# Attention and gated MLP on one core: ScalarE's work and the loads of the attention part in the order of the steps, and the chunks of last rows moved in fewer transfers

## The chip, the cores and the metric

The kernel runs on one core of one Trainium2 chip. The metric is the device time of one execution, in microseconds (us). The engines are TensorE (PE, with PEld for its weight loads), VectorE (DVE), ScalarE (ACT), GpSimd (POOL) and SyncE (SP), which here issues every DMA. Each engine works through its own list of instructions in the order in which the program was laid down for it, and waits at an instruction until what that needs is there.

## The reference

`x` is 2048 rows of 576. The reference computes

```
mod = silu(c) @ w_mod                          # six rows of 576: sa, ca, ga, sb, cb, gb
h = layernorm(x) * (1 + ca) + sa
q = h @ wq                                     # 32 heads of 128; 16 kv heads, each used by two
p = softmax(q k^T / sqrt(128)), o = p v        # k, v: the last 512 cached positions
x = x + ga * (o @ wo)
h = layernorm(x) * (1 + cb) + sb
x = x + gb * ((sigmoid(h @ w_gate) * (h @ w_up)) @ w_down)
```

All of it is float32. A product is made of split operands: each number is a rounded part (hi) and the rest (lo), and three products of parts are added.

## The kernel before, in words

The work is one long attention part and, behind it, the gated MLP. Rows stand in 4 blocks of 512, and each block in 4 tiles of 128.

**The loop of the attention part** (L708 to L724) runs over steps `n`, four for each pair of head and block, 512 steps that do scores in all. A step issues on TensorE, in this order of the code: a quarter of the q projection of a later pair (`qproj`, L337), the scores of tile n+2 (`scores`, L353), the four transposes of the probabilities of tile n (`transp`, L371), and for earlier pairs the product with `wo` (`wo_acc`, L399) and with `v` (`pv`, L384). Between them lies the chain of one tile: scores in PSUM, then DVE's row maximum (L364), ACT's exponential (L366), PE's transposes two steps on (L377), and ACT's and DVE's copies of the transposed tile as hi and lo (L380, L381). Scores and transposes share three PSUM buffers (tag `st`), so the transposes of step n+1 take the buffer that the exponential of tile n+2 has read.

**Work at given steps.** A table `at_step` gives each step further work, done ahead of the step's own (L709): loads of raw weights into four buffers (`raw`, L73); ACT's rounding of them to hi (L214 for `wq`, L239 for `wo`, L327 for `k`, L333 for `v`); POOL's lo parts (L218, L219, L243, L334) and its product of `wo` with the gate row (L433); and three times the sums for a row of `mod` (`mod_sum`, L121: ten ACT products at L126, then POOL sums). Layernorms of blocks 2 and 3 and, after the middle, of blocks 0 and 1 again also stand in this table.

**Chunks.** The MLP's weights are summed and split ahead of time in the background, in 135 chunks, one every third step: a chunk that starts at step n is loaded at n (`bg_load`), summed by POOL at n+3 (`bg_sums`), rounded by ACT at n+6 (`bg_hi`, L654), its lo part made by POOL at n+7 (`bg_lo`, L659), and stored to DRAM at n+8 (`bg_store`). There are 72 chunks "ab" of whole rows of the gate and up weights, 9 "tail" chunks with the last 32 rows of four column blocks each, and 54 "down" chunks. Their scratch lies in parts of the `x` tiles that are free at that time, three regions in turn.

**The order of the work.** A planner lays the instructions down for each engine as soon as its own model of times says that they are ready, by the order of the code where several are. `pin(i)` (L209) holds an instruction behind the one that the code issued just before it on the same engine; that one may itself be free to move. Before the change pinned are the chunks' work and the splits of `wq` and `wo`; not pinned are the loads of raw weights, the exponential, the copies at L380, L347, L394, L327 and L333, and `mod_sum`. TensorE and VectorE are not pinned in the loop in either kernel.

Of the kernel before, what the change touches and what calls it, by code (L numbers as in the profile page):

```python
# [24 lines left out]
def adaln_block_kernel(ctx: ExitStack, tc: tile.TileContext, x, k_cache, v_cache, wq, wo, w_gate, w_up, w_down,  # L25
# [54 lines left out]


# [28 lines left out]
    def mod_load(m):  # L110
        ws = []
        for j in range(2):
            w = wp.tile([P, NC, D2], F32, tag="wa", name="wm", bufs=4)
            cols = slice(m * D + j * D2, m * D + (j + 1) * D2)
            nc.sync.dma_start(w, w_mod[: NC * P, cols].rearrange("(k p) n -> p k n", p=P))
            ws.append(w)
        t = wp.tile([TAIL, D], F32, tag="h", name="wmt", bufs=4)
        nc.sync.dma_start(t, w_mod[NC * P :, m * D : (m + 1) * D])
        return ws, t

    def mod_sum(loaded):  # L121
        ws, t = loaded
        for j in range(2):
            parts = [ws[j][:, k, :] for k in range(NC)] + [t[:, j * D2 : (j + 1) * D2]]
            for k, w in enumerate(parts):
                nc.scalar.activation(w, w, AF.Copy, scale=cexp[: w.shape[0], k : k + 1])  # L126
# [16 lines left out]
    def load_x(b):  # L143
        nc.sync.dma_start(xs[b], xf[b])
# [38 lines left out]
    def ln_transpose(b, t):  # L183
# [4 lines left out]
        if b > 1:  # L188
            tc.keep_in_program_order(i)
# [6 lines left out]
        nc.scalar.activation(main[:, :NC, cols], src, AF.Copy)  # L196
        nc.vector.tensor_sub(main[:, NC:, cols], src, f32(main[:, :NC, cols]))  # L197
        nc.scalar.activation(tail[:, 0, cols], pt[:, :P], AF.Copy)
# [3 lines left out]
    def load_a(w, n0):  # L202
        raw = raw_tile([P, NC + 1, P])
        nc.sync.dma_start(raw[:, :NC, :], w[: NC * P, n0 : n0 + P].rearrange("(k p) n -> p k n", p=P))
        for s in range(2):
            nc.sync.dma_start(raw[s * TAIL : (s + 1) * TAIL, NC, :], w[NC * P :, n0 : n0 + P])
        return raw

    def pin(i):  # L209
        tc.keep_in_program_order(i)  # L210
# [21 lines left out]
    def load_b(w, n0):  # L232
        raw = raw_tile([P, D])
        nc.sync.dma_start(raw, w[n0 : n0 + P, :])
# [61 lines left out]
    NEG = {}  # L296
# [20 lines left out]
    def load_kv(cache, g):  # L317
        raw = raw_tile([P, KT, DH])
        nc.sync.dma_start(raw, cache[0, g, SK - W :, :].rearrange("(p k) d -> p k d", k=KT))
        return raw  # L320

    def prep_k(raw):
# [4 lines left out]
        nc.scalar.activation(t[:, 0, :], p, AF.Copy)  # L327
# [3 lines left out]
    def prep_v(raw):  # L331
        t = at.tile([P, 2, KT, DH], F32R, tag="vs", name="vs", bufs=2)
        nc.scalar.activation(t[:, 0], raw, AF.Copy)  # L333
# [3 lines left out]
    def qproj(b, part):  # L337
# [7 lines left out]
        if part == 3:  # L345
            t = at.tile([P, 2, BLK], F32R, tag="qt", name="qt", bufs=2)
            nc.scalar.activation(t[:, 0, :], p, AF.Copy, scale=QSCALE)  # L347
# [5 lines left out]
    def scores(n):  # L353
# [10 lines left out]
        nc.vector.tensor_reduce(NEG[b][:, i : i + 1], p, axis=AX.X, op=OP.max, negate=True)  # L364
        PP[n] = at.tile([P, W], F32, tag="pp", name="pp", bufs=2)
        nc.scalar.activation(PP[n], p, AF.Exp, bias=NEG[b][:, i : i + 1], accum_out=SUM[b][:, i : i + 1])  # L366
# [4 lines left out]
    def transp(n):  # L371
# [8 lines left out]
        nc.scalar.activation(PT[b][:, 0, :, cols], pv_, AF.Copy)  # L380
# [3 lines left out]
    def pv(b, k):  # L384
# [7 lines left out]
        if k == KT - 1:  # L392
            o = at.tile([P, 2, BLK], F32R, tag="ov", name="ov", bufs=2)
            nc.scalar.activation(o[:, 0, :], OP_[b], AF.Copy)  # L394
# [136 lines left out]
    def pair_sums(pair, t, h, ta, tb, ea, eb):  # L531
# [6 lines left out]
        for c0, src in ((0, h[0].rearrange("p (c d) -> p c d", c=2)), (2, ta), (4, h[1][:, None, hi]), (5, tb)):  # L538
            n = src.shape[1]
            nc.sync.dma_start(d[:, c0 : c0 + n, t, 0:D2], src)  # L540
            for q in range(1, 4):
                nc.sync.dma_start(d[:, c0 : c0 + n, t, 2 * P + q * TQ : 2 * P + (q + 1) * TQ], src[:, :, 2 * P :])
# [11 lines left out]
    def park_x(b):  # L554
        nc.sync.dma_start(xscr[b], xs[b])
# [12 lines left out]
    A11, A12, S1, S2, S4, S3, A22, A21 = range(8)  # L568
# [25 lines left out]
    def bg_load(k, b0):  # L594
# [16 lines left out]
        if kind == "ab":  # L611
            parts = [(slice(0, P), s * P, P, slice(f * P, (f + 1) * P))]
        else:
            parts = [(slice(q * TQ, (q + 1) * TQ), 2 * P, TQ, slice((f + q) * P, (f + q + 1) * P)) for q in range(4)]
        for rows, r0, nr, cc in parts:
            g = w_gate[:, cc].rearrange("(c r) n -> r c n", c=2)[r0 : r0 + nr]
            pin(nc.sync.dma_start(raw[rows, 0:2, :], g))
            pin(nc.sync.dma_start(raw[rows, 3, :], w_up[r0 : r0 + nr, cc]))
            pin(nc.sync.dma_start(raw[rows, 2, :], w_up[D2 + r0 : D2 + r0 + nr, cc]))
# [24 lines left out]
    def bg_pairs(k):  # L644
        r, m, hi = BG[k]
        if jobs[k][0] == "down":
            return [(0, 2, r[:, 0:2, :]), (2, 4, m[:, 0:2, :]), (4, 5, r[:, 2:3, :]), (5, 7, m[:, 2:4, :])] \
            + [(7, 8, r[:, 3:4, :])] * (jobs[k][1] == NF // 2 - 1)
        return [(0, 2, r[:, 0:2, :]), (2, 6, m), (6, 7, r[:, 2:3, :])]
# [11 lines left out]
    def bg_store(k):  # L661
        kind, f, s = jobs[k]
        hi = BG[k][2]
# [16 lines left out]
        del BG[k]  # L680
# [5 lines left out]
    for k, (n, half) in enumerate(slots):  # L686
# [4 lines left out]
        at_n(n + 8, bg_store, k)  # L691
# [16 lines left out]
    for n in range(NLO, N + 2 * TPB):  # L708
        for fn, args in at_step.pop(n, ()):  # L709
# [7 lines left out]
        if 0 <= n < N:  # L717
            transp(n)
        if ok(b - 2):
# [52 lines left out]
    for u in range(U):  # L772
        uses.append((u, 0))
        if u:
            uses.append((u - 1, 6))
        uses += [(u, a) for a in range(1, 6)]
    uses.append((U - 1, 6))
# [16 lines left out]
    WITH = {A11: 0, A12: 1, S1: 2, S2: 3, S4: 4, S3: 5, A22: 6}  # L794
# [7 lines left out]
    sd_uses = [(g, a) for g in range(GL) for a in ORDER] + [(GL, i) for i in (0, 7, 1, 4)]  # L802
# [148 lines left out]
    for u in range(U + 1):  # L951
# [23 lines left out]
        if u > 0:  # L975
# [5 lines left out]
            if g == GL:  # L981
                a, ops = (A11, ((0, A12), (7, S4))) if u % 2 else (A12, ((1, A12), (4, S4)))
# [88 lines left out]
```

## Time and profile before

| | |
|---|---|
| median of 3 runs | 3128.54 us (3126.2 to 3131.26) |
| profiled execution | 3131.72 us, span 3129.9 us, mean granted TensorE clock 0.993 |
| PE busy | 3065.7 us of the span |
| DVE, ACT, POOL busy | 2156.5, 1452.1, 1563.0 us |
| attention loop (transposes L377) | from 54.1 to 1849.4 us of the span |

The span is the time from the first to the last instruction of the profiled execution; the execution's own time is 1.8 us more. A time in the trace is counted from the span's start. A row of the timeline has start, duration, engine, line, operation, output and input; in brackets stands how long the engine sat idle before it, and what ended that. A row of waits has who waited, for whom, us in total, how often, and the longest. A row of the windows has for each engine its busy time and number of instructions in the stretch, then the granted clock of TensorE.

### The profile page before, as it was taken

The numbers are of one execution on the slowest core, as the hardware profiler recorded it, in microseconds if no ns is written. First come the engines' busy times: TensorE is split into PE (matmuls) and PEld (weight loads), VectorE is DVE, ScalarE is ACT, GpSimd is POOL, SyncE is SP. The second block draws the span as 40 slices with busy tenths as digits, with TensorE's granted clock in tenths as the row PEclk, the third lists the DMA queues.
The fourth block names the chain that finished last, engine by engine and source line by source line (L and its number), as shares of the span: only waits on it lengthen the run. The fifth ranks groups of instructions, "written<-read, shape, count | busy, mean of one in ns | idle before, by whom it ended". The sixth has DMA issues, their size and how long they took to land.

```text
span 3129.9 us, 50861 instructions
## 1 busy us (share of the span) xinstructions
PE 3065.7 (98%) x17012; PEld 2650.5 (85%) x17012; DVE 2156.5 (69%) x4202; ACT 1452.1 (46%) x3189; POOL 1563.0 (50%) x1937
## 2 busy tenths in 40 slices
PE   7999999999999999999999999999999999999998
PEld 5888888888888788888888888888888888888887
DVE  7777777777888677777777785555555665555556
ACT  4666665656555456655555543222332322322321
POOL 3666566555444336666566614554444354434444
PEclk8999999999999999999999999999999999999999
DMA  4565566555313225544444437886666776666663
GB/s 143 149 165 151 153 163 171 146 150 160 124 31 94 66 76 162 131 126 125 108 118 115 108 112 271 265 252 208 198 200 199 220 240 198 198 196 197 201 204 119
DMA packets 576740, 501.73 MB, mean 160 GB/s; under 512 B 193504, under 2 KB 456672, under 8 KB 575456
## 3 DMA queue, kind: packets, MB, share of 16 engines
q1 hardware_dynamic: 576480, 498.49, 55.3%
q8 instruction: 135, 2.21, 0.3%
q14 instruction: 125, 1.02, 0.1%
HBM read 357.83 MB, written 140.48 MB: 159 GB/s over the span
## 4 chain that ended last, share of the span: by engine, by line
PE 89%; DVE 3%; POOL 3%; DMA 2%; issue 1%; SPq 1%; ACT 1%; POOLq 0%; DVEq 0%; ACTq 0%
PE a L892 14%; PE w L251 12%; PE qp L251 12%; PE wo L251 12%; PE ot L251 10%; PE st L251 10%; PE c L892 7%; PE st L377 7%; PE b L892 4%; SPq L670 1%; DVE x L404 0%; DVE x L864 0%; DMA ts<-scr 0%; POOL hl L823 0%; PE w L762 0%
## 5 line engine op out<-in xcount | busy, mean ns | idle before, releaser
L864 DVE TENSOR_TENSOR x<-w,x 128x288 f32<-128x288 f32 x980 | 444.3, 456 | 468.3 <-PE w L251 466.4
L251 PE MATMUL wo<-wb,ov 128*128 128x288 f32 x3072 | 618.6, 309 | 4.0 <-DVE x L404 2.6
L380 ACT ACTIVATE ptt<-st 128x512 fp32r<-128x512 f32 x512 | 305.8, 597 | 616.4 <-PE st L377 616.0
L251 PEld LDWEIGHTS w<-sd,hl 128*128 128x128 f32 x3036 | 513.7, 189 | 89.4 <-POOL hl L823 4.6
L892 PE MATMUL a<-hc,sw 128*128 128x512 f32 x2016 | 583.1, 394 | 3.4 <-DVE v L1026 1.8
L251 PE MATMUL w<-sd,hl 128*128 128x288 f32 x3036 | 565.6, 296 | 3.5 <-POOL hl L823 3.1
L404 DVE SCALAR_TENSOR_TENSOR x<-wo,rs,x 128x288 f32<-128x288 f32 x1024 | 513.6, 512 | 55.8 <-PE wo L251 7.1
L364 DVE TENSOR_REDUCE neg<-st 128x1 f32<-128x512 f32 x512 | 352.7, 689 | 282.9 <-PE st L251 280.4
L251 PEld LDWEIGHTS wo<-wb,ov 128*128 128x128 f32 x3072 | 484.4, 190 | 53.8 <-DVE x L404 4.1
L251 PE MATMUL qp<-hTm,wa 128*128 128x512 f32 x1536 | 445.7, 399 | 6.6 <-DVE qt L348 4.1
L251 PE MATMUL ot<-ptt,vs 128*128 128x512 f32 x1536 | 445.0, 397 | 0.0
L251 PE MATMUL st<-kt,qt 128*128 128x512 f32 x1536 | 438.4, 393 | 2.2 <-DVE hTm L197 2.0
L892 PEld LDWEIGHTS a<-hc,sw 128*128 128x128 f32 x2016 | 355.5, 188 | 43.1 <-DVE v L1026 3.2
L381 DVE TENSOR_TENSOR ptt<-st,ptt 128x512 fp32r<-128x512 f32 x512 | 348.9, 681 | 36.2 <-ACT ptt L380 36.1
L366 ACT ACTIVATE pp<-st,neg 128x512 f32<-128x512 f32 x512 | 349.9, 683 | 37.3 <-DVE neg L364 33.9
L251 PEld LDWEIGHTS st<-kt,qt 128*128 128x128 f32 x1536 | 288.3, 188 | 65.3 <-DVE hTm L197 2.2
L377 PEld LDWEIGHTS st<-ident,pp 128*128 128x128 f32 x2048 | 254.8, 140 | 90.5 <-ACT pp L366 23.6
L377 PE MATMUL st<-ident,pp 128*128 128x128 f32 x2048 | 308.6, 273 | 17.9 <-ACT pp L366 17.6
L243 POOL TENSOR_TENSOR wb<-raw,wb 128x576 fp32r<-128x576 f32 x64 | 91.3, 1427 | 450.6 <-ACT wb L239 429.1
L892 PE MATMUL c<-hc,sw 128*128 128x512 f32 x1008 | 305.5, 395 | 3.9 <-ACT v L899 3.9
L251 PEld LDWEIGHTS qp<-hTm,wa 128*128 128x128 f32 x1536 | 262.6, 189 | 34.1 <-DVE qt L348 5.2
L251 PEld LDWEIGHTS ot<-ptt,vs 128*128 128x128 f32 x1536 | 260.7, 189 | 23.5 <-DVE ptt L381 0.2
(150 smaller groups left out, 3854.6 us busy)
## 6 DMA issues: line engine op xcount, KB each, us to landing
sw<-wsc SPq DMA_DIRECT2D x504, 320.0 KB, 3.3
sd<-dsc SPq DMA_DIRECT2D x249, 288.0 KB, 2.9
wsc<-x SPq DMA_DIRECT2D x72, 448.0 KB, 3.5
raw<-in_A_wo_dram SPq DMA_DIRECT2D x64, 288.0 KB, 3.0
dsc<-x SPq DMA_DIRECT2D x51, 336.0 KB, 3.0
raw<-in_A_wq_dram SPq DMA_DIRECT2D x64, 256.0 KB, 2.9
wsc<-x SPq DMA_DIRECT2D x54, 256.0 KB, 3.4
dsc<-x SPq DMA_DIRECT2D x126, 96.0 KB, 2.5
```

The lines of the kernel that those rows point to most:

```text
L243: pin(nc.gpsimd.tensor_sub(sp[:, 1, :], raw, f32(sp[:, 0, :])))
L251: nc.tensor.matmul(p, l, r, start=first and n == 0, stop=last and n == len(pairs) - 1)
L364: nc.vector.tensor_reduce(NEG[b][:, i : i + 1], p, axis=AX.X, op=OP.max, negate=True)
L366: nc.scalar.activation(PP[n], p, AF.Exp, bias=NEG[b][:, i : i + 1], accum_out=SUM[b][:, i : i + 1])
L377: nc.tensor.transpose(p[:, k * P : (k + 1) * P], PP[n][:, k * P : (k + 1) * P], ident)
L380: nc.scalar.activation(PT[b][:, 0, :, cols], pv_, AF.Copy)
L381: nc.vector.tensor_sub(PT[b][:, 1, :, cols], pv_, f32(PT[b][:, 0, :, cols]))
L404: nc.vector.scalar_tensor_tensor(xv, p, RS[b][:, i : i + 1], xv, op0=OP.mult, op1=OP.add)
L670: pin(nc.sync.dma_start(wsc[f + q][to * TQ : (to + 1) * TQ, a:b, 4, :], src[rows]))
L864: nc.vector.tensor_add(acc, p, acc)
L892: nc.tensor.matmul(p, l, r, start=first and n == 0, stop=n == len(pairs) - 1, skip_group_check=not first)
```

## The change

1. `keep_order` pins an instruction while a flag is set; it is set from step 8 to step 511. It is put around every ACT instruction of the loop that was not pinned and around the DMAs of `load_a`, `load_b`, `load_kv`, `load_x`, `mod_load`, `park_x` and `pair_sums`. So in these steps ACT's and SP's lists are the order of the code, whole.
2. The exponential gets a function of its own, `expo`, called behind `transp(n)`; in the code it stood ahead of it.
3. Loads stand closer to their use: `wq` 4 steps before its rounding (before: 8), `k` 6 (8), `v` 6 (8), `wo` 3 steps before POOL's product (4) and 5 before its rounding (7). POOL's product with the gate row is 2 steps ahead of the rounding (3). POOL's lo part of `wo` comes one step after the rounding (same step).
4. Chunks: a tail chunk is loaded in 4 DMAs (before: 12) and stored in 24 (48), half of them one step later. The order of the seven operands in DRAM is changed, so that every chunk has two groups of operands (before: three for "ab" and "tail", four for "down"; in both kernels one more for the last three "down" chunks): fewer and longer ACT and POOL instructions in `bg_hi` and `bg_lo`, fewer store DMAs. In the MLP only the slots from which operands are read are renumbered.

```diff
+    def keep_order(i):
+        if held[0]:
+            tc.keep_in_program_order(i)
...
-        nc.scalar.activation(PP[n], p, AF.Exp, bias=NEG[b][:, i : i + 1], accum_out=SUM[b][:, i : i + 1])
+        ST[n] = p
+
+    def expo(n):
+        b, i = divmod(n, TPB)
+        PP[n] = at.tile([P, W], F32, tag="pp", name="pp", bufs=2)
+        keep_order(nc.scalar.activation(PP[n], ST.pop(n), AF.Exp, bias=NEG[b][:, i : i + 1],
+                                        accum_out=SUM[b][:, i : i + 1]))
...
-        nc.scalar.activation(PT[b][:, 0, :, cols], pv_, AF.Copy)
+        keep_order(nc.scalar.activation(PT[b][:, 0, :, cols], pv_, AF.Copy))
...
-                nc.scalar.activation(w, w, AF.Copy, scale=cexp[: w.shape[0], k : k + 1])
+                keep_order(nc.scalar.activation(w, w, AF.Copy, scale=cexp[: w.shape[0], k : k + 1]))
...
-        nc.sync.dma_start(raw, w[n0 : n0 + P, :])
+        keep_order(nc.sync.dma_start(raw, w[n0 : n0 + P, :]))
...
-        at_n(max(q_first(hh) - 16, NLO), load_q, hh)
+        at_n(max(q_first(hh) - 12, NLO), load_q, hh)
...
-            at_n(n - 15, load_k, gg)
+            at_n(n - 13, load_k, gg)
...
-            at_n(n - 10, load_v, gg)
+            at_n(n - 8, load_v, gg)
...
-        at_n(n - 7, load_o, hh)
-        at_n(max(n - 3, 1), scale_o, hh)
+        at_n(n - 5, load_o, hh)
+        at_n(max(n - 2, 1), scale_o, hh)
         at_n(n, split_o, hh)
-        at_n(n, split_o_lo, hh)
+        at_n(min(n + 1, o_first(hh) - 1), split_o_lo, hh)
...
+        for slot, w, r0 in ((0, w_gate, 2 * P), (1, w_gate, D2 + 2 * P), (3, w_up, 2 * P), (2, w_up, D2 + 2 * P)):
+            src = w[r0 : r0 + TQ, f * P : (f + 4) * P].rearrange("r (q n) -> q r n", q=4)
+            pin(nc.sync.dma_start(raw[:, slot, :], src))
...
-        return [(0, 2, r[:, 0:2, :]), (2, 6, m), (6, 7, r[:, 2:3, :])]
+        plain = [(7, 8, r[:, 3:4, :])] if jobs[k][0] == "down" and jobs[k][1] == NF // 2 - 1 else []
+        return [(0, 3, r[:, 0:3, :]), (3, 7, m)] + plain
...
-            for q in range(4):
+            for q in (0, 1) if part == 0 else (2, 3):
                 rows = slice(q * TQ, (q + 1) * TQ)
                 for to in range(4):
-                    for a, b, lo in bg_pairs(k):
-                        src = lo if to % 2 else hi[:, a:b, :]
+                    for a, b, src in bg_pairs(k) if to % 2 else [(0, 7, hi)]:
...
+        at_n(n + 9, bg_store, k, 1)
...
+        if n == 8:
+            held[0] = True
+        if n == N:
+            held[0] = False
...
             transp(n)
+        if 0 <= n + 2 < N:
+            expo(n + 2)
```

More of the change, by code (lines that the diff above doesn't have):

```diff
@@ L79, in adaln_block_kernel, with pin @@
     ident = const.tile([P, P], F32, name="ident")
+    def pin(i):
+        tc.keep_in_program_order(i)
+    held = [False]
+    def keep_order(i):
+        if held[0]:
+            tc.keep_in_program_order(i)
     csb = const.tile([P, NC + 1], F32, name="csb")
@@ L143, in load_x @@
     def load_x(b):
-        nc.sync.dma_start(xs[b], xf[b])
+        keep_order(nc.sync.dma_start(xs[b], xf[b]))
     LN, HH = {}, {}
@@ L295, in adaln_block_kernel @@
     QT, SUM, RS, PP, PT, OT, OP_, QP = {}, {}, {}, {}, {}, {}, {}, {}
-    NEG = {}
+    NEG, ST = {}, {}
     seq = []
@@ L318, in load_kv @@
         raw = raw_tile([P, KT, DH])
-        nc.sync.dma_start(raw, cache[0, g, SK - W :, :].rearrange("(p k) d -> p k d", k=KT))
+        keep_order(nc.sync.dma_start(raw, cache[0, g, SK - W :, :].rearrange("(p k) d -> p k d", k=KT)))
         return raw
@@ L332, in prep_v @@
         t = at.tile([P, 2, KT, DH], F32R, tag="vs", name="vs", bufs=2)
-        nc.scalar.activation(t[:, 0], raw, AF.Copy)
+        keep_order(nc.scalar.activation(t[:, 0], raw, AF.Copy))
         nc.gpsimd.tensor_sub(t[:, 1], raw, f32(t[:, 0]))
@@ L564, in adaln_block_kernel @@
         at_n(n1 + 21 + 6 * t, early_sums, t)
-    A11, A12, S1, S2, S4, S3, A22, A21 = range(8)
+    A11, A12, A22, S1, S2, S4, S3, A21 = range(8)
     wsc = [dram.tile([P, 7, 5, P], F32, tag=f"wsc{f}", name=f"wsc{f}") for f in range(NF)]
@@ L611, in bg_load @@
         if kind == "ab":
[L612 to L619, printed above, removed]
+            r0, cc = s * P, slice(f * P, (f + 1) * P)
+            g = w_gate[:, cc].rearrange("(c r) n -> r c n", c=2)[r0 : r0 + P]
+            pin(nc.sync.dma_start(raw[:, 0:2, :], g))
+            pin(nc.sync.dma_start(raw[:, 3, :], w_up[r0 : r0 + P, cc]))
+            pin(nc.sync.dma_start(raw[:, 2, :], w_up[D2 + r0 : D2 + r0 + P, cc]))
+            return
+        for slot, w, r0 in ((0, w_gate, 2 * P), (1, w_gate, D2 + 2 * P), (3, w_up, 2 * P), (2, w_up, D2 + 2 * P)):
+            src = w[r0 : r0 + TQ, f * P : (f + 4) * P].rearrange("r (q n) -> q r n", q=4)
+            pin(nc.sync.dma_start(raw[:, slot, :], src))
     def bg_sums(k):
@@ L659, in bg_lo, with bg_store @@
             pin(nc.gpsimd.tensor_sub(v.bitcast(F32R), v, hi[:, a:b, :]))
-    def bg_store(k):
+    def bg_store(k, part):
         kind, f, s = jobs[k]
+        if part and kind != "tail":
+            return
         hi = BG[k][2]
         if kind == "tail":
-            for q in range(4):
+            for q in (0, 1) if part == 0 else (2, 3):
                 rows = slice(q * TQ, (q + 1) * TQ)
                 for to in range(4):
-                    for a, b, lo in bg_pairs(k):
-                        src = lo if to % 2 else hi[:, a:b, :]
+                    for a, b, src in bg_pairs(k) if to % 2 else [(0, 7, hi)]:
                         pin(nc.sync.dma_start(wsc[f + q][to * TQ : (to + 1) * TQ, a:b, 4, :], src[rows]))
@@ L679, in bg_store @@
                 pin(nc.sync.dma_start(to[1][:, a:b, :], lo))
-        del BG[k]
+        if part or kind != "tail":
+            del BG[k]
     STEP = 3
@@ L772, in adaln_block_kernel @@
     for u in range(U):
-        uses.append((u, 0))
+        uses.append((u, A11))
         if u:
-            uses.append((u - 1, 6))
-        uses += [(u, a) for a in range(1, 6)]
-    uses.append((U - 1, 6))
+            uses.append((u - 1, A22))
+        uses += [(u, a) for a in (A12, S1, S2, S4, S3)]
+    uses.append((U - 1, A22))
     at_use = [0]
@@ L801, in adaln_block_kernel @@
     GL = 2 * NG - 1
-    sd_uses = [(g, a) for g in range(GL) for a in ORDER] + [(GL, i) for i in (0, 7, 1, 4)]
+    sd_uses = [(g, a) for g in range(GL) for a in ORDER] + [(GL, i) for i in (0, 7, 1, 2)]
     at_sd = [0]
```

41 lines of the change are left out of this document (18 added, 23 removed).

## The prediction

> **What bounds the kernel now.** I read the page first, then TensorE's waits in the attention loop, then a table of windows around the longest of them, then the timeline just ahead of each.
>
> ```profile
> span 3129.9 us, 50861 instructions
> PE 3065.7 (98%) x17012; PEld 2650.5 (85%) x17012; DVE 2156.5 (69%) x4202; ACT 1452.1 (46%) x3189; POOL 1563.0 (50%) x1937
> ```
>
> TensorE is busy but for 64 us, and the change takes no matmul away. So all it can win is TensorE's idle time, and what its clock loses after that. In the part that the flag covers, from 60 us to the end of the loop, these are all the waits:
>
> ```profile
> PE st L377 <- ACT pp L366: 17.6, 8, 4.1
> PE qp L251 <- DVE qt L348: 2.6, 1, 2.6
> PE wo L251 <- DVE ov L395: 1.0, 1, 1.0
> PE wo L251 <- DVE x L404: 0.9, 1, 0.9
> PE st L251 <- DVE ptt L381: 0.2, 1, 0.2
> ```
>
> The eight waits of the transposes for an exponential are the only large group. Four of them are 3.5 to 4.1 us long:
>
> ```profile
> core 0: us, PE busy (x) PEld busy (x) DVE busy (x) ACT busy (x) POOL busy (x), PEclk, DMA share, GB/s
> 530.00:545.00 15.00, 11.16 (x56) 9.47 (x55) 6.82 (x12) 6.76 (x16) 12.27 (x19) 0.89 0.53 150
> 1030.00:1045.00 15.00, 10.92 (x54) 9.03 (x53) 6.76 (x14) 4.38 (x10) 5.68 (x6) 0.89 0.38 104
> 1496.00:1511.00 15.00, 11.53 (x57) 9.77 (x56) 7.02 (x13) 6.50 (x18) 13.25 (x26) 0.89 0.45 112
> 1667.00:1682.00 15.00, 11.53 (x59) 9.74 (x58) 7.31 (x15) 6.45 (x18) 13.24 (x27) 0.89 0.46 116
> 538.20:541.60 3.40, 3.40 (x14) 3.11 (x14) 1.98 (x4) 2.58 (x7) 3.16 (x5) 0.50 0.39 112
> 1000.90:1004.30 3.40, 3.40 (x20) 2.95 (x21) 3.40 (x7) 1.47 (x4) 2.92 (x3) 1.00 0.54 130
> ```
>
> Idle time in the four windows of 15 us is 3.84, 4.08, 3.47 and 3.47 us, 14.9 in sum. The clock is 0.89 in each, though, which is 0.11 x 15 = 1.65 us of full speed lost, 6.6 in sum; the fifth row shows where, 3.4 us at half clock right behind a wait. The last row lies behind the one wait of 2.6 us (of `qp`): no clock is lost there. [...]
>
> Who kept the exponential? ACT's timeline ahead of the third and the second wait:
>
> ```profile
> 1495.33 0.20 ACT L366 ACTIVATION_READ_ACCUMULATOR pp<-st,neg 128x1 f32 x1
> 1499.62 0.36 ACT L654 ACTIVATE x<-x 128x192 fp32r<-128x192 f32 x1 [4.09 <-POOL x L630]
> 1502.36 0.54 ACT L654 ACTIVATE x<-x 128x192 fp32r<-128x192 f32 x2 [2.37 <-POOL x L633]
> 1502.80 0.58 ACT L380 ACTIVATE ptt<-st 128x512 fp32r<-128x512 f32 x1
> ...
> 1037.13 0.63 ACT L333 ACTIVATE vs<-raw 128x512 fp32r<-128x512 f32 x1 [6.32 <-DMA raw<-in_A_v_cache_dram]
> ```
>
> ACT sits 6.5 us at a chunk's rounding for POOL's sums of the same chunk, with copy and exponential queued behind it. The code sets three steps between these sums and this rounding; here the rounding was laid down so early that POOL had not begun. At 1037 it is the rounding of `v` before its load has landed, at 536 a chunk again:
>
> ```profile
> 535.51 0.45 POOL L641 TENSOR_TENSOR extra<-x,extra 128x128 f32<-128x128 f32 x1
> 536.00 0.63 ACT L654 ACTIVATE x<-extra 128x512 fp32r<-128x512 f32 x1 [5.04 <-POOL extra L641]
> 550.06 0.60 PE L377 MATMUL st<-ident,pp 128*128 128x128 f32 x4
> ```
>
> `extra` is the region of every third chunk; this one is chunk 44, by the code loaded at step 136, summed at 139 and rounded at 142. The transposes of step 142 run at 550. So ACT waited at 531 for work that the code asks for at about 549, when POOL's sums (done at 536) would have been there for 13 us. ACT ran ahead of the code, and POOL was, if anything, ahead of it too.
>
> **The change part by part.** *ACT in the order of the steps* takes all of this class away, if POOL and SP keep within three steps of the code. Of the 17.6 us, one wait has another cause, DVE's maximum:
>
> ```profile
> 1023.23 0.69 ACT L366 ACTIVATE pp<-st,neg 128x512 f32<-128x512 f32 x1 [2.39 <-DVE neg L364]
> ```
>
> It and the other DVE waits stay (DVE is not held). The wait of TensorE there I read as 1.0 us. So 17.6 - 1.0 + 6.6 = 23.2 us are to be had.
>
> What does the order itself cost? An ordinary step:
>
> ```profile
> 516.57 0.60 PE L377 MATMUL st<-ident,pp 128*128 128x128 f32 x4
> 517.21 0.60 ACT L380 ACTIVATE ptt<-st 128x512 fp32r<-128x512 f32 x1 [2.27 <-PE st L377]
> 517.70 0.68 ACT L366 ACTIVATE pp<-st,neg 128x512 f32<-128x512 f32 x1
> 519.89 0.60 PE L377 MATMUL st<-ident,pp 128*128 128x128 f32 x4
> ```
>
> ACT is already in the order copy, exponential; the move of `expo` behind `transp` alters nothing here. The exponential ends at 518.38, and the next transposes, which need its buffer, start at 519.89: 1.5 us to spare. With the 2.27 us that ACT idles ahead of the copy, a step has room for 3.8 us of other ACT work.
>
> ```profile
> 233.09 1.38 ACT L126 ACTIVATE wm<-wm,cexp 128x288 f32<-128x288 f32 x3
> ...
> 490.92 1.13 ACT L654 ACTIVATE x<-x 128x256 fp32r<-128x256 f32 x3
> L214 ACT ACTIVATE wa<-raw 128x640 fp32r<-128x640 f32 x64 | 46.9, 734 | 0.0
> L239 ACT ACTIVATE wb<-raw 128x576 fp32r<-128x576 f32 x64 | 43.5, 680 | 0.0
> ```
>
> Added up from the table of steps, the fullest ordinary step (splits of `wq`, `k` and `wo` and a chunk, three times 128x256 at most) has 0.73 + 0.60 + 0.68 + 1.13 = 3.1 us; the 0.60 for `k` is that of the copy at L380, which has its shape. It fits, though with 0.7 us only.
>
> `mod_sum` does not fit. It has ten products, now in one row at steps 23, 55 and 87 (20 + 32k + 3): 10 x 1.38 / 3 = 4.6 us, 0.8 over the room. Step 55 has a chunk's rounding as well, 1.1 more. And these are steps with the copy of `ov` behind the exponential (every fourth), which comes late to `wo_acc`; some 0.5 us each. Bound from above: 0.8 + 1.9 + 0.8 + 1.5 = 5.0 us. Bound from below: 0, since the planner, which knows of the queue, may put `wo`, `pv` and `qp` matmuls ahead of the late transposes. I take 3, nearer the upper end, because the scores behind it need the same PSUM buffers. No single wait is over 2.4 us, so by the two rows above none should cost clock; were the loss in proportion (6.6 us per 14.9), it would be 1.3 us more.
>
> *SP in the order of the steps, and loads nearer to their use.*
>
> ```profile
> SPq L234 <- POOL wb L243: 172.4, 19, 26.3
> SPq L679 <- POOL x L659: 141.1, 135, 4.7
> raw<-in_A_wo_dram SPq DMA_DIRECT2D x64, 288.0 KB, 3.0
> L377 PE MATMUL st<-ident,pp x2048: 270/272/477, 54.1 to 1849.4; 128*128 128x128 f32 x187
> ```
>
> The first row is a load of `wo` at the head of SP's list for up to 26 us: by the table, one step in 16 wants a fifth raw buffer while there are four. With the new distances never more than four are in use, so this wait goes, and with it a cause of late loads. A step is (1849.4 - 54.1) / 512 = 3.5 us. A load lands in 3.0, so three steps (10.5 us) leave 7.5 us, and the rounding of `wo` has five. Cost: nothing, as long as SP is less than two steps late; what then is late first is POOL's product with the gate row. On the other side, the stores' waits for POOL (second row) now stand ahead of all later loads; 4.7 us is the longest, inside the margin. [...]
>
> *Fewer, larger chunk transfers and instructions.*
>
> ```profile
> L670 SPq DMA_DIRECT2D wsc<-x x360: 302/427/1667, 167.2 to 1269.5; - x180
> L654 ACT ACTIVATE x<-x 128x192 fp32r<-128x192 f32 (+4 forms) x399 | 132.3, 385 | 16.0 <-POOL x L630 8.2 <-POOL x L633 2.4 <-POOL x L641 2.3
> L654 ACT ACTIVATE x<-extra 128x192 fp32r<-128x192 f32 (+1 forms) x63 | 30.0, 477 | 7.4 <-POOL extra L641 5.0 <-POOL extra L633 2.4
> ACT ptt L380 <- PE st L377: 616.0, 459, 3.5
> POOL wb L243 <- ACT wb L239: 429.1, 52, 25.3
> ```
>
> A tail chunk's 48 stores hold SP for 48 x 0.427 = 20.5 us, six steps; 24 hold it for 10.2 us over two steps (7.0 us). ACT's roundings fall from 462 to 135 x 2 + 3 = 273; at some 0.2 us each (three of 0.36 on average make 1.13 us; two would do the same elements in about 0.95) this saves 38 us of ACT and about as much of POOL. Both lie under time in which these engines wait anyway (616 us of ACT for TensorE, 429 of POOL for ACT), so they are worth nothing by themselves. If TensorE were ever to wait for them they would be a gain, so this part has no cost that I can find.
>
> *The MLP* only reads other slots; its work, 1.2 ms of it, I take as unchanged. Its order may be laid out a little differently; I allow 2 us either way.
>
> **Sum.** -23.2 + 3.0 = -20.2 us. The profiled execution took 3131.7 us, so 3111.5 by its own time. It stood 3.2 us above the median of the runs (3128.5), so I predict 3108.
>
> **The rivals.**
>
> *POOL is late by the code's order too.* Then ACT, held, waits at the same three chunks' roundings, and only the wait for `v` and the small ones go: 23.2 - 3 x (3.6 + 1.65) = 7.5 us, less 3 for `mod_sum`: 3124. For it: POOL's pins are as before. Against it: at 536 POOL was 13 us ahead of the code, and it waits 429 us for ACT. Chance 0.12.
>
> *The full steps are too full.* Every eight steps the splits stand in one step, and with a chunk's rounding 0.7 us is left; if a wait for POOL or for PE's `k` transposes eats 1.2 us there, TensorE loses 0.5 us in each of 60 steps, 30 us, of which a third would have a chunk: 10 to 15 us, so 3118 to 3123. For it: the order is rigid where the planner used to fill gaps. Against it: today the same splits stand in one step without a wait of TensorE. Chance 0.08.
>
> *SP falls behind and it gets slower.* A tail's 24 stores (10.2 us), the landing that the next load into its region waits for and other loads (2 to 5 us) put SP two steps behind; all loads now queue behind the stores. If the lag passes four steps at the load of `wo`, ACT's rounding of it waits, and everything of the step behind it: one wait like today's per tail chunk, 9 x 5.2 = 47 us, 3155. It decides from 14 us of lag; I count 7 to 8. Before, SP was held for 20.5 us by the same chunks and the waits found were not there. Chance 0.07.
>
> *The new order of ACT makes the planner lay out DVE and PE otherwise,* and DVE waits such as the 2.6 us of `qt` multiply: ten of them would eat the gain, 3130 to 3135. Nothing in the trace speaks for so many. Chance 0.05.
>
> **Chances and range.** The forecast has 0.68 (3100 to 3116: from all DVE waits gone too, 4.7 us, and `mod_sum` free, to `mod_sum` at its bound and one long wait left). 0.2% of 3128.5 us is 6.3 us, about what a measurement of this kernel can tell from no change, so faster means below 3122. That takes the forecast and half of the first two rivals: 0.68 + 0.10 = 0.78. The other half of these and a little of the last are the same: 0.12. Slower: 0.10. To leave out no more than two in ten the range takes in the first two rivals: 3098 to 3126.
>
> **What would show it.** Right: in the loop no wait of TensorE over 3 us, no slice with a clock under 1.00, the row of L377 waiting for L366 down from 17.6 to under 6 us, and what is left of it at three places 32 steps apart (near 135, 250 and 360 us); no wait of a `raw` load for L243 beyond a step; SP's stores of tails (L670's successor) at 216; ACT's roundings at 273. Wrong: ACT still idle over 2 us ahead of a chunk's rounding (the first rival); small waits of L377 at every eighth step (the second); SP's queue over three steps behind after a tail, with POOL's L433 waiting for a DMA (the third); DVE named in most of TensorE's waits (the last).

## The result, and the profile after

The changed kernel takes 3099.46 us (median of 4 runs, 3098.51 to 3100.44) against 3128.74 us before: a ratio of 0.9906, with a 95% interval of 0.9889 to 0.9924. The forecast was 3108 us, inside a range of 3098 to 3126; the gain is 29 us, where 20 had been worked out. How the parts of the change bring it is not what the forecast said.

The page of the changed kernel (its profiled execution took 3100.44 us):

```profile
span 3098.6 us, 49831 instructions
...
PE 3051.9 (98%) x17012; PEld 2643.8 (85%) x17012; DVE 2153.9 (70%) x4202; ACT 1437.3 (46%) x3000; POOL 1537.9 (50%) x1748
...
PEclk9999999999999999999999999999999999999999
```

TensorE's waits in the same stretch as before, from 60 us to the end of the loop. The transposes are now L388, the exponential L376, the copy L391, the matmul helper L257, the chunk's rounding L665 and its lo part L670:

```profile
PE ot L257 <- DVE ptt L392: 2.6, 3, 0.9
PE st L388 <- ACT pp L376: 2.2, 4, 1.3
PE wo L257 <- DVE ov L406: 1.0, 1, 1.0
PE st L257 <- DVE ptt L392: 0.2, 1, 0.2
```

No wait is longer than 1.3 us, and the waits for the exponential have gone from 17.6 to 2.2 us. The trace has no half clock inside the loop. The row of the transposes' line gives the ends of the stages:

```profile
L388 PE MATMUL st<-ident,pp x2048: 269/272/330, 49.6 to 1821.5; 128*128 128x128 f32 x187
```

The loop took 1849.4 - 54.1 = 1795.3 us before and takes 1821.5 - 49.6 = 1771.9 now, 23.4 less. Ahead of it 54.1 - 49.6 = 4.5 us went, behind it (3129.9 - 1849.4) - (3098.6 - 1821.5) = 3.4. That is the 31.3 us between the two spans.

The 4.5 us ahead of the loop lie at its doorstep. First the windows of the kernel before, then of the changed one:

```profile
42.00:60.00 18.00, 10.93 (x46) 7.95 (x47) 15.19 (x26) 11.41 (x31) 6.61 (x7) 0.81 0.09 25
```

```profile
42.00:60.00 18.00, 12.03 (x65) 8.89 (x64) 15.37 (x28) 10.22 (x26) 9.19 (x9) 1.00 0.08 23
```

Before, TensorE ran here at a clock of 0.81, 0.19 x 18 = 3.4 us of full speed lost; now at 1.00. The two orders of TensorE are the same up to 40 us. This part goes with the later load of `wq`: in the seven kernels of this document that have it the loop starts at 49.6 to 51.4 us, in the seven without it at 52.9 to 54.5. In the MLP the gaps of TensorE add up to the same in both (15.8 and 15.9 us); only the stretches at half clock differ, 5.1 us lost against 1.7.

### The profile page after: what moved, and what is told of

Its sections match the earlier page's. It is cut to its first block, busy times and chain, and to the rows that moved or that the text cites. A ratio compares the mean times of both kernels' runs of the same rounds, so it can differ in the third digit from the quotient of the medians.

```text
span 3098.6 us, 49831 instructions
## 1 busy us (share of the span) xinstructions
PE 3051.9 (98%) x17012; PEld 2643.8 (85%) x17012; DVE 2153.9 (70%) x4202; ACT 1437.3 (46%) x3000; POOL 1537.9 (50%) x1748
## 4 chain that ended last, share of the span: by engine, by line
PE 93%; DVE 2%; DMA 1%; POOL 1%; ACT 1%; issue 1%; SPq 0%; DVEq 0%; POOLq 0%; ACTq 0%
PE a L912 14%; PE qp L257 13%; PE wo L257 13%; PE w L257 12%; PE ot L257 11%; PE st L257 11%; PE st L388 7%; PE c L912 7%; PE b L912 3%; POOL hl L843 0%; PE w L782 0%; DVE x L884 0%; PE st L331 0%; ACT wm L136 0%; POOL vs L848 0%
## 5 line engine op out<-in xcount | busy, mean ns | idle before, releaser
L257 PE MATMUL wo<-wb,ov 128*128 128x288 f32 x3072 | 616.4, 309 | 3.1 <-DVE x L415 1.7
L391 ACT ACTIVATE ptt<-st 128x512 fp32r<-128x512 f32 x512 | 305.8, 597 | 642.2 <-PE st L388 642.2
L257 PEld LDWEIGHTS w<-sd,hl 128*128 128x128 f32 x3036 | 512.9, 188 | 89.2 <-POOL hl L843 5.3
L257 PE MATMUL w<-sd,hl 128*128 128x288 f32 x3036 | 564.2, 295 | 3.9 <-POOL hl L843 3.5
L257 PEld LDWEIGHTS wo<-wb,ov 128*128 128x128 f32 x3072 | 482.7, 189 | 52.4 <-DVE x L415 2.8
L257 PE MATMUL qp<-hTm,wa 128*128 128x512 f32 x1536 | 445.5, 399 | 4.2 <-ACT wa L220 1.4
L257 PE MATMUL ot<-ptt,vs 128*128 128x512 f32 x1536 | 444.8, 396 | 2.6 <-DVE ptt L392 2.6
L257 PE MATMUL st<-kt,qt 128*128 128x512 f32 x1536 | 437.7, 393 | 0.2 <-DVE ptt L392 0.2
L376 ACT ACTIVATE pp<-st,neg 128x512 f32<-128x512 f32 x512 | 350.2, 684 | 41.5 <-DVE neg L370 40.9
L257 PEld LDWEIGHTS st<-kt,qt 128*128 128x128 f32 x1536 | 287.7, 188 | 62.6 <-DVE ptt L392 1.0
L388 PEld LDWEIGHTS st<-ident,pp 128*128 128x128 f32 x2048 | 254.1, 139 | 72.3 <-ACT pp L376 5.0
L388 PE MATMUL st<-ident,pp 128*128 128x128 f32 x2048 | 306.5, 272 | 2.2 <-ACT pp L376 2.2
L257 PEld LDWEIGHTS qp<-hTm,wa 128*128 128x128 f32 x1536 | 262.4, 189 | 30.7 <-DVE qt L354 2.1
L257 PEld LDWEIGHTS ot<-ptt,vs 128*128 128x128 f32 x1536 | 259.6, 188 | 26.2 <-DVE ptt L392 3.4
L670 POOL TENSOR_TENSOR x<-x,x 128x384 fp32r<-128x384 f32 (+3 forms) x183 | 178.1, 984 | 165.2 <-ACT x L665 165.1
```

The source lines that it names most:

```text
L257: nc.tensor.matmul(p, l, r, start=first and n == 0, stop=last and n == len(pairs) - 1)
L376: keep_order(nc.scalar.activation(PP[n], ST.pop(n), AF.Exp, bias=NEG[b][:, i : i + 1], accum_out=SUM[b][:, i : i + 1]))
L388: nc.tensor.transpose(p[:, k * P : (k + 1) * P], PP[n][:, k * P : (k + 1) * P], ident)
L391: keep_order(nc.scalar.activation(PT[b][:, 0, :, cols], pv_, AF.Copy))
L670: pin(nc.gpsimd.tensor_sub(v.bitcast(F32R), v, hi[:, a:b, :]))
```

## The experiments

The change has four parts: ScalarE held in the order of the steps (with `expo` behind `transp`), SyncE held, the new distances, the new chunks. Twelve kernels took them apart. All differ from one of the two kernels only by the edits named, and all compute everything. `expo` stands behind `transp` in every kernel with a hold, those that hold SyncE and not ScalarE (e2, e4, e7) included; that move has no run of its own. Ratios are to the kernel before; 0.001 of it is 3.1 us.

| kernel | ACT held | SP held | new distances | new chunks | us | ratio, 95% interval |
|---|---|---|---|---|---|---|
| before | | | | | 3128.7 | |
| e1 | x | | | | 3144.3 | 1.0056 [1.0039, 1.0072] |
| e3 | | | | x | 3145.4 | 1.0057 [1.0042, 1.0072] |
| e7 | | x | | | 3133.5 | 1.0021 [1.0011, 1.0031] |
| e5 | | | `wq` load only | | 3133.0 | 1.0017 [1.0007, 1.0026] |
| e6 | | | x | | 3111.0 | 0.9944 [0.9929, 0.9959] |
| e10 | | | lo of `wo` only | | 3113.9 | 0.9955 [0.994, 0.997] |
| e2 | | x | x | | 3103.1 | 0.9919 [0.9905, 0.9934] |
| e4 | | x | x | x | 3105.2 | 0.9925 [0.991, 0.994] |
| e9 | x | | | x | 3109.8 | 0.9942 [0.9927, 0.9957] |
| e8 | x | x | | x | 3104.5 | 0.9925 [0.991, 0.994] |
| e11 | x | x | x | | 3125.8 | 0.9989 [0.998, 0.9998] |
| after | x | x | x | x | 3099.5 | 0.9906 [0.9889, 0.9924] |
| e12 | x | x | x | x, `mod_sum` spread | 3101.1 | 0.9917 [0.99, 0.9933] |

### ScalarE held, and nothing else

```diff
+    held = [False]
+    def keep_order(i):
+        if held[0] and i.ins.engine == mybir.EngineType.Activation:
+            tc.keep_in_program_order(i)
...
-        nc.scalar.activation(PT[b][:, 0, :, cols], pv_, AF.Copy)
+        keep_order(nc.scalar.activation(PT[b][:, 0, :, cols], pv_, AF.Copy))
...
+        if 0 <= n + 2 < N:
+            expo(n + 2)
```

> The kernel before with ScalarE alone held in the order of the steps, the exponential behind the transposes; SyncE's loads not held, old distances, old chunks. If ScalarE running ahead of the code is the cause of the long waits: the wait of the transposes for the exponential falls from 17.6 us to 2 to 5 us (what is left at the three mod_sum steps), the loop shortens by 16 to 24 us, time 3102 to 3112. If late loads and a late POOL are the cause (a fifth raw buffer is wanted every 16 steps), ScalarE waits for POOL at the same places: wait over 10 us, time over 3120. If the chunks' transfers are: about 3128.

Measured: 3144.3 us, 0.56% slower. The forecast gave this edit the whole gain. ScalarE's waits in the loop (a row each, by whom it waited for):

```profile
ACT ptt L391 <- PE st L388: 601.5, 461, 3.7
ACT x L666 <- DMA wsc<-x: 56.3, 17, 9.0
```

The waits of a chunk's rounding for POOL's sums are gone, as the forecast said they would be: none over 1 us is left. In their place stands a wait that was 1.4 us in sum before: the rounding waits for a store of an earlier chunk. ScalarE's timeline at the first long one:

```profile
283.92 0.20 ACT L376 ACTIVATION_READ_ACCUMULATOR pp<-st,neg 128x1 f32 x1
291.91 0.42 ACT L666 ACTIVATE x<-x 128x256 fp32r<-128x256 f32 x1 [7.79 <-DMA wsc<-x]
292.59 0.83 ACT L666 ACTIVATE x<-x 128x512 fp32r<-128x512 f32 x2 [0.26 <-DMA wsc<-x]
293.32 0.58 ACT L391 ACTIVATE ptt<-st 128x512 fp32r<-128x512 f32 x1
```

The copy and the exponential stand behind that rounding as they stood behind the early ones before. TensorE's waits for the exponential have grown from 17.6 us:

```profile
PE st L388 <- ACT pp L376: 26.7, 13, 6.3
```

Where does the store come from? The rounded operands of the chunks lie in two places in turn, so the chunk two places on overwrites them. A chunk that starts at step n is stored at n+8, and the one two places on is rounded at n+6+6 = n+12. The code leaves four steps, 14 us, to send everything off and land it. An unheld ScalarE could put its copies and exponentials ahead of a rounding that the stores would hold up; a held one cannot. None of the explanations on record ahead of this run had named that wait.

### The new chunks, and nothing else

```diff
+        return [(0, 3, r[:, 0:3, :]), (3, 7, m)] + plain
...
+            for q in (0, 1) if part == 0 else (2, 3):
...
+        at_n(n + 9, bg_store, k, 1)
```

> The kernel before with the new chunks alone (tail chunks in 4 loads and 24 stores over two steps, two groups of operands); nothing held, old distances. If ScalarE's order is the cause: within 6 us of the kernel before, long waits at other places, since the planner's times change a little. If the 20 us that a tail chunk's stores hold SyncE are the cause: 10 us or more faster.

Measured: 3145.4 us, as much slower as the hold by itself. ScalarE's waits:

```profile
ACT vs L333 <- DMA raw<-in_A_v_cache_dram: 16.2, 9, 6.6
ACT x L653 <- POOL x L631: 13.0, 3, 4.3
ACT x L653 <- POOL extra L642: 5.0, 1, 5.0
ACT x L653 <- POOL x L636: 4.8, 2, 2.4
ACT x L653 <- POOL x L642: 4.8, 1, 4.8
```

These are the waits of the kernel before, and more of them: an unheld ScalarE at roundings that are not ready. TensorE has the same order as before, instruction for instruction, so the loss is waiting: 23.8 us for the exponential (17.6 before), and 15.4 us of the loop lost at half clock (6.8 before). Fewer instructions did not help: ScalarE starts 12 chunks more than a step ahead of the code, 8 before (a rounding's start, against the transposes of the step that asks for it).

### SyncE's order and the load of `wq`, each alone

```diff
+        if held[0] and i.ins.engine == mybir.EngineType.SP:
+            tc.keep_in_program_order(i)
```

> The kernel before with SyncE held in the order of the steps, old distances, old chunks, ScalarE not held (the exponential called behind the transposes). Raw buffer as the cause: no gain, 3122 to 3145, the waits of raw loads at the head of SyncE's list stay above 200 us. Held order of SyncE as the cause: 3100 to 3110.

```diff
-        at_n(max(q_first(hh) - 16, NLO), load_q, hh)
+        at_n(max(q_first(hh) - 12, NLO), load_q, hh)
```

> The kernel before with one number changed: the raw wq weights are loaded 12 steps ahead of the projection instead of 16, so that no more than four raw buffers are ever wanted. Nothing held, old chunks. If the load that waits for a fifth raw buffer at the head of SyncE's list is the cause of the long waits: SyncE's waits of raw loads fall from over 300 us to under 100, the waits of the transposes for the exponential from 17.6 us to under 6, time 3102 to 3114. If the held order of SyncE's list is the cause: 3122 or more, long waits remain.

Measured: 3133.5 and 3133.0 us, each about 0.2% slower. The two test SyncE's share: the raw buffers that a load waits for, which the forecast called a cause of late loads. The load of `wq` alone is a poor test of them, since SyncE's waits at raw loads in the loop fall only from 439 us in sum to 382, where under 100 was expected. The faster kernels e8, e9 and e10, further down, settle it: there these waits are 484, 567 and 452 us, more than before. They are not what costs time. In the kernel with everything but the new distances (e8, 3104.5 us), the two largest are:

```profile
SPq L213 <- PE st L331: 156.9, 22, 11.1
SPq L240 <- POOL wb L249: 114.6, 31, 11.2
```

That is 271 us of raw loads standing at full buffers, and the kernel is 0.75% faster all the same.

### The new distances, alone and with SyncE held

```diff
-            at_n(n - 15, load_k, gg)
+            at_n(n - 13, load_k, gg)
...
-        at_n(n - 7, load_o, hh)
-        at_n(max(n - 3, 1), scale_o, hh)
+        at_n(n - 5, load_o, hh)
+        at_n(max(n - 2, 1), scale_o, hh)
...
-        at_n(n, split_o_lo, hh)
+        at_n(min(n + 1, o_first(hh) - 1), split_o_lo, hh)
```

> The kernel before with all the new distances (wq, k, v, wo loads, the product with the gate row, the low part of wo), nothing held, old chunks. Raw buffer as the cause: 3100 to 3112, within 4 us of the run with the wq distance alone. Held order of SyncE as the cause: 3120 or more.

With SyncE held as well, beside the distances:

```diff
+        if held[0] and i.ins.engine == mybir.EngineType.SP:
+            tc.keep_in_program_order(i)
```

> The kernel before with SyncE's loads alone held in the order of the steps and with the new distances between loads and uses; ScalarE not held (the exponential is called behind the transposes), old chunks. If ScalarE's early chunk work is the cause: long waits remain, over 10 us, time 3115 to 3130. If loads that come late are: time 3100 to 3110.

Measured: 3111.0 us with all the distances and nothing else, 3103.1 with SyncE held as well. The part that the forecast costed at nothing takes off 17.5 us by itself, with ScalarE free. It is no matter of TensorE's own order: that is the same in this kernel and the one with the load of `wq` alone, instruction for instruction, and the two are 22 us apart. One number of it does most of that:

```diff
-        at_n(n, split_o_lo, hh)
+        at_n(min(n + 1, o_first(hh) - 1), split_o_lo, hh)
```

> The kernel before with one number changed: POOL's low part of wo is asked for one step later than its rounding and not in the same step. All new distances together took 18 us off, and the later load of wq alone nothing. Theory: POOL has stood still at the low part of wo for ScalarE's rounding (429 us in sum) and this makes its sums of chunks late, so that an unheld ScalarE that runs ahead finds them late: with the low part a step later 3105 to 3118 us, the wait of POOL for the rounding of wo under 150 us, and the sum of TensorE's waits for the exponential under 8 us. Rival: it is the other distances (loads of k, v, wo and the scaling of wo) that do it: 3124 to 3132 us, whatever POOL waits.

Measured: 3113.9 us. POOL's waits in this kernel:

```profile
POOL wa L218 <- ACT wa L214: 266.7, 47, 27.5
POOL x L659 <- ACT x L654: 188.8, 61, 7.1
...
POOL wb L243 <- ACT wb L239: 41.3, 8, 17.5
```

POOL still waits, but elsewhere. Before, it stood 429.1 us at the low part of `wo`, which the code asked for in the step of its rounding, and 58.6 us at `wa`. The sums of a chunk queue behind whatever POOL stands at. POOL's timeline in the kernel before, ahead of the rounding at 1499.62 us that the prediction shows, has such a wait of 9.76 us; the second row is the first step of the sums (L630), which that rounding waits for:

```profile
1493.68 1.42 POOL L243 TENSOR_TENSOR wb<-raw,wb 128x576 fp32r<-128x576 f32 x1 [9.76 <-ACT wb L239]
...
1498.99 1.16 POOL L630 TENSOR_TENSOR x<-x,gate 128x192 f32<-128x192 f32 x2
```

With the low part one step later POOL comes to the sums earlier. For each of the 135 chunks the trace gives the end of its last sum and the start of its first rounding. The median of the time between was 8.3 us before, and 9 chunks had under 1 us; here they are 12.3 us and 4. ScalarE runs ahead as it did (8 chunks start more than a step ahead of the code in both kernels, by up to 3.5 steps before and 3.2 here), but now POOL is mostly done. What is left in TensorE's list, and ScalarE's timeline at the longest wait:

```profile
PE st L377 <- ACT pp L366: 5.3, 2, 4.1
```

```profile
1031.63 0.63 ACT L333 ACTIVATE vs<-raw 128x512 fp32r<-128x512 f32 x1 [6.34 <-DMA raw<-in_A_v_cache_dram]
```

The three long waits for chunks are gone; the one for `v`, which this edit doesn't touch, is still there.

### Everything but the hold of ScalarE

```diff
-        if held[0]:
+        if held[0] and i.ins.engine == mybir.EngineType.SP:
```

> The changed kernel with ScalarE not held (but SyncE held, new distances, new chunks, the exponential called behind the transposes). If ScalarE's order is the cause: most of the gain is lost, 3115 or more, waits of the transposes for the exponential over 8 us. If loads and chunks are the cause: within 5 us of the changed kernel, 3095 to 3105.

Measured: 3105.2 us. Without the hold that the forecast made the whole cause, 23.5 of the 29 us are there; its interval overlaps that of the changed kernel, so what the hold adds on top of the rest is not resolved. TensorE waits 3.9 us for the exponential, in seven pieces of 1.1 us at most.

### Everything but the distances, and then the hold of ScalarE with the chunks alone

```diff
-        at_n(min(n + 1, o_first(hh) - 1), split_o_lo, hh)
+        at_n(n, split_o_lo, hh)
```

(and the other distances of the change set back likewise, the two stores of chunks left as changed)

> The changed kernel (ScalarE and SyncE held, new chunks) with the old distances alone. Raw buffer as the cause: the whole gain is lost, 3122 to 3150, waits of the transposes for the exponential over 10 us. If the order of either list is the cause: within 6 us of the changed kernel, 3096 to 3106.

And the kernel before with ScalarE's hold and the new chunks:

```diff
+        if held[0] and i.ins.engine == mybir.EngineType.Activation:
+            tc.keep_in_program_order(i)
...
+        return [(0, 3, r[:, 0:3, :]), (3, 7, m)] + plain
...
+        at_n(n + 9, bg_store, k, 1)
```

> The kernel before with two parts of the change: ScalarE held in the order of the steps, and the new chunk transfers (24 stores of a tail chunk over two steps). SyncE's other loads are left to the planner and all distances are old. Alone, each of the two parts cost 0.6%. Theory: an unheld ScalarE runs ahead to roundings that are not ready, and a held one waits for the stores of a tail chunk; the hold cures the first and the fewer stores cure the second, so the two together win what neither wins alone: 3100 to 3112 us, and no wait of ScalarE over 4 us for a store of a chunk. Rival: the hold of SyncE's loads is a needed third part (with it and these two the time was 3104.5): 3120 us or more, with waits of ScalarE for DMA.

Measured: 3104.5 and 3109.8 us. The second has only the two parts that cost 15 to 18 us each when alone, and the two together win 18. ScalarE's and TensorE's waits in it:

```profile
ACT x L665 <- DMA wsc<-x: 4.5, 2, 2.8
```

```profile
PE st L388 <- ACT pp L376: 5.2, 7, 2.1
```

The 56.3 us at stores are 4.5, and no rounding waits for POOL: in each of the 135 chunks the sums are done at least 3.2 us ahead. POOL waits 371 us at the low part of `wo` here, against 429 before. So POOL is on time by the code's order, even with the old distances. At the three chunks of the long waits it was late only for a ScalarE that came too early: in the kernel before its sums there were done 12.8 to 14.1 us ahead of the transposes of the step. (Elsewhere in that kernel the sums of some chunks ended behind those transposes, by up to 9.5 us, and no long wait of TensorE stands there.)

### Everything but the chunks

```diff
-            for q in (0, 1) if part == 0 else (2, 3):
+            for q in range(4):
...
-        at_n(n + 8, bg_store, k, 0)
-        at_n(n + 9, bg_store, k, 1)
+        at_n(n + 8, bg_store, k)
```

> The changed kernel with the old chunk transfers (48 stores of a tail chunk in one step, three pairs of roundings a chunk); ScalarE and SyncE held, the new distances. Theory: the held ScalarE meets the stores again that have not landed: after tail chunks it waits for a store, and TensorE for it, as in the run with ScalarE held alone; 3108 to 3135 us, with a wait of ScalarE's rounding for a store of a chunk over 20 us in sum. Rival: with the new distances that wait is gone whatever the stores are, and the chunk part is worth nothing: 3096 to 3104 us.

Measured: 3125.8 us: 26 of the 29 us are lost again. SyncE's timeline at the third tail chunk, first and last rows of its 48 stores, then ScalarE's over the same time:

```profile
365.06 4.39 SPq L682 DMA_DIRECT2D wsc<-x  x4
370.39 0.30 SPq L682 DMA_DIRECT2D wsc<-extra  x1
...
391.98 0.42 SPq L682 DMA_DIRECT2D wsc<-extra  x1
392.45 0.43 SPq L682 DMA_DIRECT2D wsc<-x  x1
```

```profile
384.81 0.63 ACT L339 ACTIVATE vs<-raw 128x512 fp32r<-128x512 f32 x1
391.83 0.42 ACT L666 ACTIVATE x<-x 128x256 fp32r<-128x256 f32 x1 [6.39 <-DMA wsc<-x]
...
393.21 0.58 ACT L391 ACTIVATE ptt<-st 128x512 fp32r<-128x512 f32 x1
```

The stores run from 365.1 to 392.9 us, 27.8 us where the code leaves 14, and the held rounding sits 6.4 us until those that read what it overwrites have landed. In sum:

```profile
PE st L388 <- ACT pp L376: 16.3, 14, 4.3
```

```profile
ACT x L666 <- DMA wsc<-x: 40.4, 16, 6.6
```

In the changed kernel the same place reads so, SyncE's first and last rows of the 24 stores, then ScalarE's:

```profile
356.24 4.06 SPq L682 DMA_DIRECT2D wsc<-x  x2
...
373.18 0.43 SPq L682 DMA_DIRECT2D wsc<-extra  x1
```

```profile
375.30 0.63 ACT L339 ACTIVATE vs<-raw 128x512 fp32r<-128x512 f32 x1
375.82 1.04 ACT L665 ACTIVATE x<-x 128x384 fp32r<-128x384 f32 x2
```

17.4 us from the first to the last, and the rounding comes 2.2 us behind them, without a wait. The chunk part is what makes the hold bearable.

### The products of `mod_sum` spread over four steps

```diff
-        at_n(n + 3, lambda m=m: mod_sum(wm[m]))
+        for part in range(4):
+            at_n(n + 3 + part, lambda m=m, part=part: mod_sum(wm[m], part))
```

> The changed kernel with the ten products of a modulation weight, which stand in one row in ScalarE's order at three steps, spread over four steps. Theory: the three waits of the transposes at 128, 242 and 355 us (0.34, 1.27 and 0.34 us) are these products; they go, and the time falls by 1 to 3 us, to 3096 to 3099. Rival: the planner lays out the rest otherwise and the three waits turn up elsewhere: within 2 us of the changed kernel.

Measured: 3101.1 us, no better than the changed kernel. The cause was right. Of the waits of the transposes (L390 here) only the fourth is left:

```profile
PE st L390 <- ACT pp L378: 0.2, 1, 0.2
```

The loop from step 8 on is 3.1 us shorter (1746.1 us, 1749.2 in the changed kernel). The MLP, which nothing was done to, took 2.8 us longer in this profile, with 5.1 us lost at half clock against 1.7. A gain of this size is below what these runs resolve, and no version beat the changed kernel.

## Why the prediction was right, and where not

**The bound: right.** TensorE's waits for the exponential and the half clock behind them were the gain: of the 23.4 us of the loop, 17.6 - 2.2 = 15.4 are these waits and 6.8 the clock (four stretches of 3.4 us, 1.7 each). The other waits moved from 4.7 to 3.8 us.

**"ACT in the order of the steps takes all of this class away": the step that failed.** It does take it away, but alone (e1) it puts another in its place, which costs more: 3144.3 us where 3102 to 3112 was expected. The condition in that sentence, "if POOL and SP keep within three steps of the code", was not met by SyncE: I had the number (48 stores, 20.5 us, six steps) and used it only for loads that queue behind the stores. I didn't ask who overwrites what is being stored. The rounding two chunks on does, and its limit is four steps.

**"They are worth nothing by themselves ... no cost that I can find" (chunks): wrong both ways.** Alone they cost 18 us (e3); with ScalarE held they decide over 26 (e11 against after) to 36 us (e1 against e9, 1.0056 to 0.9942). I reckoned with instruction time under cover, and the part acts by when the last store is through. The 24 stores also save less than half the time: 12.4 to 13.4 us of issuing per tail chunk, added up from the trace (20 to 22 us for the 48), not 10.2, since one of them takes 0.54 us to issue on average, where one of the 48 took 0.44:

```profile
L682 SPq DMA_DIRECT2D wsc<-x x144: 331/589/1128, 163.3 to 1237.7; - x144
L682 SPq DMA_DIRECT2D wsc<-extra x72: 303/434/1049, 167.5 to 1238.4; - x72
```

**"Cost: nothing" (order of loads, distances): rightly no loss in the whole change, and a gain not seen.** The distances alone win 17.5 us (e6), and the low part of `wo` a step later 14 (e10). The row of 429.1 us, POOL waiting for `wb`, was in the prediction, read as spare time of POOL. It was also the reason why POOL came late to the sums. The raw buffers, to which the forecast gave "a cause of late loads", were not it (e8, e9, e10), nor does their wait go: raw loads still stand 219 us in the changed kernel, up to 19.7 us at a time, and nothing is seen to pay for it. With the later loads no loss shows here; the kernel with only the load of `wq` later is 0.17% slower, for a reason that was not followed.

**`mod_sum`: right in place, a little large.** The ten products take 4.27 us (235.94 to 240.21 in the timeline at step 55); the transposes wait at 128.2, 241.5 and 354.9 us, 0.34 + 1.27 + 0.34 = 1.95 us where 3 was taken. The products' estimate was 4.6 us.

```profile
235.00 1.04 ACT L665 ACTIVATE x<-x 128x384 fp32r<-128x384 f32 x2
235.94 1.80 ACT L136 ACTIVATE wm<-wm,cexp 128x288 f32<-128x288 f32 x4
...
239.78 0.53 ACT L136 ACTIVATE wmt<-wmt,cexp 64x288 f32<-64x288 f32 x1
240.21 0.58 ACT L391 ACTIVATE ptt<-st 128x512 fp32r<-128x512 f32 x1
```

**The sum.** 31.3 us of span against 20.2: 3 us more in the loop, 4.5 ahead of it, 3.4 behind. The 4.5 us, where the planner lays out TensorE otherwise from 40 us on, go with the load of `wq` and were left out altogether. Most of the 3.4 us has no cause in the change that I can show: over the fourteen profiles the MLP took 1249 to 1260 us, and which stretches fall to half clock differs from one to the next. The measured 3099.5 us lies inside the range, and 0.5 us below the 3100 to 3116 to which the forecast gave 0.68. That the sum came so near is in part luck: the hold, to which it gave the whole gain, loses 16 us alone, the part priced at nothing turns that round, and 7.9 of the 31.3 us lie where no gain was forecast.

**The rivals.** *POOL late by the code's order too* is refuted by e9 and after: no rounding waits for POOL. *The full steps too full* is refuted: nothing recurs every eight steps in TensorE's list. *DVE laid out otherwise* did not come about in the changed kernel, though a wait of 2.0 to 3.7 us for `qt` stands in seven of the twelve others (e1, e3, e5, e6, e7, e9, e10). *SP falls behind* was the right mechanism with the wrong victim: in e1 and e11 the 48 stores do hold up ScalarE, by way of a region in use and not of a late load of `wo`. The change itself contains the cure, and it stayed faster.

**The marks.** No wait over 3 us, no half clock in the loop, L388 under 6 us at the three places named, 144 + 72 = 216 stores, 273 roundings (228 + 45): all as said. One was not: no wait of a `raw` load for L243 (now L249) beyond a step, 3.5 us. SyncE's rows have 9.9 and 8.5:

```profile
SPq L325 <- POOL wb L249: 12.4, 4, 9.9
SPq L240 <- POOL wb L249: 8.5, 1, 8.5
```

The marks that were right would have stood just as well beside a wrong account of the causes; e2 and e4, with ScalarE free, show the first three of them nearly as well.

**What stays open.** Why the two lone parts' plans (e3, e7) come out slower than the old plan is seen only in its effect: more early roundings of chunks in e3 (12 against 8), longer waits of ScalarE for loads of `v` in e7 (27.4 us against 16.4); the planner's choice behind it was not followed. Nor do the intervals tell after, e2, e4 and e8 apart by cause: each has a cure for the early roundings, and what after has on top is worth 3.7 to 5.8 us by the medians. The loop takes 1771.9 us in after and in e8, 1772.6 in e2 and 1776.0 in e4. So with ScalarE held and the new chunks the new distances win nothing more in the loop; what e8 lacks is 3.8 us ahead of it, and 3.0 us behind it.

## What to carry to other kernels

Holding an engine in the order of the code moves the wait from what it took too early to whatever in that order is truly late (in e1 to stores, 56.3 us in sum); so before adding a hold, list for each held instruction everything it needs, the landing of a store whose source it overwrites included, with the steps that the code allows and the time that it takes. When two edits each make it slower, that says nothing yet on the two together (e1 and e3 lose 0.56 and 0.57%, e9 wins 0.58). And a long wait of an engine that isn't the bound is no mere slack (POOL's 429.1 us at the low part of `wo`): what stands behind it in the queue can be late by that wait (9.76 us ahead of the sums at 1498.99), and it costs as soon as another engine asks for it early.

## What the runs showed of the hardware

The prediction read from two rows that a wait of 2.6 us costs no clock. The MLP of the kernel before has the opposite: half clock from 2535.0 to 2541.8 us, around the end of this wait:

```profile
2535.72 0.80 PE L892 MATMUL c<-hc,sw 128*128 128x512 f32 x1 [2.75 <-ACT v L899]
```

In the kernel with the low part of `wo` a step later, the same wait for `qt` costs clock too (TensorE's timeline, then the window behind the wait):

```profile
994.75 0.50 PE L251 MATMUL qp<-hTm,wa 128*128 128x512 f32 x1 [2.61 <-DVE qt L348]
```

```profile
996.00:999.40 3.40, 3.40 (x13) 2.87 (x12) 3.21 (x7) 1.49 (x5) 2.93 (x3) 0.50 0.69 191
```

Everything but the chunks (e11) shows it even behind a wait of 2.07 us, with another of 0.40 us close by: the clock is 0.50 from 395.4 to 398.8 us. Over the fourteen profiles, of 34 waits between 1.9 and 3 us in loop and MLP 23 met 3.4 us or more at half clock within 2 us; of those over 3 us all did (in before and after by themselves 2 of 3, and 4 of 4). In each of these traces every stretch at half clock, but for the one at the very end of the span, lasts 3.41 us or a multiple, and all of them start on one grid of 3.413 us over the whole 3.1 ms. In the kernel before, the four of the loop start at 538.19, 1039.95, 1504.16 and 1674.83 us, which is 147, 136 and 50 times 3.413 us apart. The same wait costs clock or not as it falls: the one for `qt` cost none with 2.64 us in the kernel before, and 3.4 us at half clock with 2.61 us in the kernel above. So a wait of 2 to 3 us is here to be priced at about 1 us over its length, an estimate from these profiles (23/34 x 1.7).

In these traces the grid says more than the length of a wait does. Cut the fourteen by it, from 60 us to 20 us ahead of the end, and take the stretches of 3.41 us at full clock: all 49 in which TensorE idled for over 0.55 of the 3.41 us (1.9 us) were followed by half clock, 9 of the 24 with 0.45 to 0.55, and 3 of 12288 with less (in before and after by themselves 6 of 6, 1 of 3 and none of 1759). So such a stretch was not idle from end to end where half clock followed: in the kernel before, the one from 2531.58 us held 2.02 us of idle time, and the clock was 0.50 behind it. And a wait that the grid cuts in two cost nothing: of the one of 2.64 us the stretch from 998.99 us held 1.86, and the clock behind it was 1.00.
